# Last stage of an adaLN block on one core: weights stationary and 512 tokens moving in six of seven block products

## Chip, cores and metric

The kernel runs on one core of a Trainium2 chip. The metric is device time in microseconds (us) of one execution; before the change it is 539.46 us, the median of three runs (539.36 to 539.9).

## What is computed

One transformer block on 2048 tokens of width 512, in float32, with a modulation vector from `silu(c) @ w_mod`:

```python
h = _layernorm(x) * (1 + ca) + sa
x = x + ga * _A_ref(h, wqkv, wo)              # linear attention, 32 heads
h = _layernorm(x) * (1 + cb) + sb
x = x + gb * (((h @ w_gate) * (h @ w_up)) @ w_down)   # F = 1376
```

## The kernel before

The work is written out by hand, engine by engine; no scheduler reorders it. Tokens come in four chunks of 512, each as four tiles of 128 tokens by 512 columns (`xts[chunk][j]`). Every matrix operand is split into a high and a low half of type float32r (`split`, L195), and a product of two matrices is three matmuls: high·high, high·low, low·high.

The feed-forward part runs in blocks of 128 hidden features (`block`, L1176). Chunks 2 and 3 have their down projection last, after all blocks, in `Down.run` (L1515), which is the last stage. It multiplies the hidden features of chunks 2 and 3 (`a11`, `a12` of chunk 2, `a21`, `a22` of chunk 3; left and right are even and odd feature tiles) by `w_down` (`b11`, `b12`, `b21`, `b22`) by Winograd's form of Strassen's scheme: seven products of blocks instead of eight. Left sums are `s1` to `s4`, right sums `t1` to `t4`. Each product has 5 pairs of feature tiles, three of them a sixth pair of 96 features (`odd`). In the order in which they run, they are called P1 to P7 here:

| product | left, right | pairs |
|---|---|---|
| P1 | a11, b11 | 5 |
| P2 | a12, b21 | 6 |
| P3 | s2, t2 | 5 |
| P4 | s1, t1 | 5 |
| P5 | s3, t3 | 6 |
| P6 | s4, b22 | 6 |
| P7 | a22, t4 | 6 |

Before, the tokens are stationary: for each of the four token tiles of a product, 128 tokens by 128 features sit in the array and the weights' 256 output columns move. P1, P3, P5 and P7 use two PSUM banks (`C`), two token tiles to a bank, with three 256-wide matmuls per pair and tile (`mm`, L1448). P2, P4 and P6 use four banks (`A`) and put high and low weights side by side into one 512-wide matmul, beside one 256-wide one (`mm_wide`, L1458). After each product VectorE adds the PSUM banks to x in SBUF (`add`, L1521); what Winograd's scheme shares between outputs comes out of PSUM by keeping sums in the banks. P7 runs tile by tile in the order j = 0, 2, 1, 3; tiles 0 and 1 share one bank, 2 and 3 the other.

Around the products, `h_split` (L1419) and `h_next` (L1425) make left halves: ScalarE copies a high half (`kh`), VectorE subtracts it for the low half (`kl`); in `h_next` VectorE also forms the s2 or s4 sum just ahead (L1417). Right halves were made in earlier blocks, parked in DRAM, and come back in `w_fetch` (L1395). SP issues every DMA of the kernel in order, and each DMA uses one of eight semaphores in turn, so that at most eight are in flight. Each engine works its queue in order.

`stow` (L996) and the lifts earlier in the kernel already use the way of turning that matters here: VectorE's transpose turns 32x32 blocks, and DMAs through DRAM put blocks in place.

Of the kernel before, what the change touches and what calls it, by code (L numbers as in the profile page):

```python
# [24 lines left out]
def tile_adaln_block(  # L25
# [27 lines left out]
    xv = x[0].rearrange("(c p j) d -> c j p d", p=P, j=NJ)  # L53
    ov = out[0].rearrange("(c p j) d -> c j p d", p=P, j=NJ)
# [56 lines left out]
    def load(src, tag):  # L111
        raw = B(tag, (P, *src.shape[1:]))[:src.shape[0]]
        nc.sync.dma_start(raw, src)
        return raw

    def load_x(ch):
        return [load(xv[ch, j], "x") for j in range(NJ)]
# [823 lines left out]
    def evac(ch, dn, js=range(NJ), last=False, cols=((0, D),)):  # L941
        for j in js:
            xt = xts[ch][j]
            for a, b in cols:
                nc.vector.tensor_tensor(xt[:, a:b], dn[j][:, a:b], xt[:, a:b], op=ALU.add)  # L945
                if last:
                    nc.sync.dma_start(ov[ch, j, :, a:b], xt[:, a:b])
# [214 lines left out]
    def copy(out, x):  # L1162
        nc.scalar.activation(out, x, AF.Copy)  # L1163
# [126 lines left out]
    banks, others = [], []  # L1290
# [18 lines left out]
    def ffn():  # L1309

        m = 0
        for g, (cs, fs) in enumerate(groups):
# [19 lines left out]
        wide_down = Down((2, 3), m, draws.pop(m))  # L1332
        wide_down.planned()
# [14 lines left out]
    class Down:  # L1348

        def __init__(self, cs, m, odd):  # L1350
            self.cs, self.m, self.odd = cs, m, odd
# [4 lines left out]
            self.raw, self.t = {}, {}  # L1356

# [100 lines left out]
        def mm_wide(self, bs, j, pairs, start):  # L1458

            a, b = j * P, (j + 1) * P  # L1460
            for (h, l), w in pairs:
                k = h.shape[0]
                nc.tensor.matmul(bs[j], h[:, a:b], w[:k].rearrange("p t c -> p (t c)"), start=start, stop=False, skip_group_check=True)  # L1463
                nc.tensor.matmul(bs[j][:, :HALF], l[:, a:b], w[:k, 0], start=False, stop=False, skip_group_check=True)
                start = False

        def product(self, bs, js, left, right, start, odd=None):
            pairs = [(self.parts[i][left, "split"], self.w[right, i]) for i in range(self.NI)]
            if odd:
                pairs.append((self.h[LATE[0]][odd[0]], self.w["odd", odd[1]]))  # L1470
            for j in js:
                if len(bs) == NJ:
                    self.mm_wide(bs, j, pairs, start)
                else:
                    self.mm(bs, j, pairs, start and j % 2 == 0)
# [38 lines left out]

        def run(self):  # L1515

            c0, c1 = self.cs
            x = lambda c, half, j: xts[c][j][:, half * HALF:(half + 1) * HALF]
            A, C = banks, others[:2]

            def add(c, half, bs, js, store=None):  # L1521
                for j in js:
                    parts = [bs[j][:, :HALF], bs[j][:, HALF:]] if bs is A else [self.part(bs, j)]
                    for ps in parts:
                        nc.vector.tensor_tensor(x(c, half, j), x(c, half, j), ps, op=ALU.add)
                    if store:
                        a, b = store
                        nc.sync.dma_start(ov[c, j, :, a:b], xts[c][j][:, a:b])

            lo, hi, js = (0, 1), (2, 3), range(NJ)  # L1530
            pairs = range(self.NI)
            last = self.NI - 1
# [305 lines left out]
```

## Time and profile before

| | |
|---|---|
| median of 3 runs | 539.46 us |
| the profiled execution's own time | 539.58 us |
| its span, first to last instruction | 537.9 us |
| last stage, P1's first matmul to P7's last | 478.86 to 534.61 us |
| mean granted TensorE clock | 1.000 |
| VectorE, ScalarE, GpSimd busy | 76%, 55%, 30% of the span |
| DMA | 109.21 MB, mean 203 GB/s |

PE is TensorE's matmul side, PEld its weight loads, DVE VectorE, ACT ScalarE, POOL GpSimd, SP the engine that issues DMAs. In a timeline a row gives start, length, engine, line, operation and tiles, with "xN" for merged neighbours and in brackets the idle time before it and what ended it. A matmul's own length is modelled and overlaps the next one; pace is read from starts. In the row of a group, the first number behind the bar is its busy time, the second the mean length of one in ns.

### The profile page before, as it was taken

What the parts mean: (1) busy time and instruction counts of PE and PEld (TensorE: products, weight loads), DVE (VectorE), ACT (ScalarE), POOL (GpSimd) and SP (SyncE); (2) the same over time, 40 slices, a digit from 0 to 9 for tenths busy, and PEclk for the clock granted to TensorE, in tenths of its full rate; (3) what the DMA queues carried; (4) which work ended last, traced back from release to release, by engine and by line L of the source; (5) the groups of instructions that cost most, each with busy time, mean ns of one, the idle gap of its engine ahead of it and who ended that gap; (6) DMA issues with size and microseconds to landing.
All of it is one profiled execution on the core that took longest, in us unless ns stands there. A gap on an engine that the chain in (4) does not pass through costs nothing.

```text
span 537.9 us, 8026 instructions
## 1 busy us (share of the span) xinstructions
PE 532.6 (99%) x2549; PEld 444.7 (83%) x2549; DVE 408.1 (76%) x701; ACT 297.7 (55%) x564; POOL 160.0 (30%) x170
## 2 busy tenths in 40 slices
PE   8999999999999999999999999999999999999997
PEld 7888888888888878878888888887888888889997
DVE  7997879999989888779766576996556564669772
ACT  3696877648587765577684545454434334246030
POOL 2001010010021220076696577747532322210000
PEclk9999999999999999999999999999999999999999
DMA  8902427310165165947869596794289998689222
GB/s 283 387 35 92 144 98 216 98 60 2 45 195 194 41 209 147 310 143 228 279 197 319 207 323 224 216 372 120 74 300 334 388 389 315 229 278 392 83 77 81
DMA packets 86396, 109.21 MB, mean 203 GB/s; under 512 B 10897, under 2 KB 41617, under 8 KB 86353
## 3 DMA queue, kind: packets, MB, share of 16 engines
q1 hardware_dynamic: 86352, 108.70, 60.3%
q8 instruction: 20, 0.33, 0.3%
q14 instruction: 24, 0.19, 0.1%
HBM read 65.93 MB, written 42.73 MB: 202 GB/s over the span
## 4 chain that ended last, share of the span: by engine, by line
PE 99%; DVE 0%; issue 0%
PE bank L1158 27%; PE acc L875 8%; PE acc L1158 7%; PE acc L1455 6%; PE bank L209 4%; PE bank L211 4%; PE bank L210 4%; PE bank L1463 3%; PE acc L416 3%; PE acc L418 3%; PE acc L417 3%; PE acc L1242 3%; PE acc L1241 3%; PE acc L1243 3%; PE bank L958 2%; PE bank L960 2%
## 5 line engine op out<-in xcount | busy, mean ns | idle before, releaser
L1158 PE MATMUL bank<-h,w 128*128 128x512 f32 (+1 forms) x630 | 145.4, 389 | 0.0
L1158 PEld LDWEIGHTS bank<-h,w 128*128 128x128 f32 (+1 forms) x630 | 117.0, 186 | 26.1 <-DVE u L1220 0.2
L1163 ACT ACTIVATE bank<-bank 128x512 f32<-128x512 f32 (+1 forms) x30 | 17.5, 583 | 74.0 <-PE bank L1158 73.8
L197 DVE TENSOR_TENSOR kl<-u,kh 128x512 fp32r<-128x512 f32 (+1 forms) x38 | 26.3, 736 | 23.9 <-ACT kh L196 21.9
L265 POOL TENSOR_TENSOR rstd<-ve,half 128x2 f32<-128x2 f32 (+3 forms) x13 | 11.8, 911 | 107.8 <-DVE ve L264 44.5
L209 PE MATMUL bank<-w,h 128*128 128x512 f32 x104 | 40.8, 392 | 0.0
L211 PE MATMUL bank<-w,h 128*128 128x512 f32 x104 | 40.6, 391 | 0.0
L210 PE MATMUL bank<-w,h 128*128 128x512 f32 x104 | 40.5, 390 | 0.0
L1158 PE MATMUL acc<-h,w 128*128 128x512 f32 x168 | 38.7, 389 | 0.0
L197 POOL TENSOR_TENSOR w<-raw,w 128x512 fp32r<-128x512 f32 (+1 forms) x15 | 22.2, 1483 | 53.4 <-ACT w L196 47.8
L875 PE MATMUL acc<-w,xh 128*128 128x512 f32 x120 | 37.1, 390 | 0.0
L1158 PEld LDWEIGHTS acc<-h,w 128*128 128x128 f32 x168 | 31.5, 188 | 6.5
L945 DVE TENSOR_TENSOR x<-acc,x 128x512 f32<-128x512 f32 x40 | 26.5, 686 | 12.8 <-PE acc L1243 11.1
L1120 POOL TENSOR_TENSOR w<-raw,w 128x256 fp32r<-128x256 f32 (+3 forms) x22 | 23.9, 1084 | 37.4 <-ACT w L1113 33.2
L1455 PE MATMUL acc<-w,kh 128*128 128x256 f32 (+1 forms) x176 | 31.8, 283 | 0.0
L1120 POOL TENSOR_TENSOR w<-t,w 128x512 fp32r<-128x512 f32 (+1 forms) x22 | 30.2, 1372 | 0.0
L1455 PEld LDWEIGHTS acc<-w,kh 128*128 128x128 f32 (+1 forms) x176 | 27.5, 192 | 0.2
L875 PEld LDWEIGHTS acc<-w,xh 128*128 128x128 f32 x120 | 22.4, 188 | 4.6
L416 PE MATMUL acc<-kh,xh 128*128 128x512 f32 x64 | 25.2, 394 | 0.0
L418 PE MATMUL acc<-kl,xh 128*128 128x512 f32 x64 | 25.0, 391 | 0.0
L417 PE MATMUL acc<-kh,xl 128*128 128x512 f32 x64 | 25.0, 390 | 0.0
L1241 PE MATMUL acc<-w,kh 128*128 128x512 f32 x64 | 24.9, 389 | 0.0
(258 smaller groups left out, 1325.5 us busy)
## 6 DMA issues: line engine op xcount, KB each, us to landing
right<-w SPq DMA_DIRECT2D x56, 256.0 KB, 3.6
w<-right SPq DMA_DIRECT2D x56, 256.0 KB, 5.1
raw<-in_w_mod_dram SPq DMA_DIRECT2D x24, 256.0 KB, 3.9
raw<-in_B_w_down_dram SPq DMA_DIRECT2D x20, 256.0 KB, 4.2
down_t<-w SPq DMA_DIRECT2D x20, 256.0 KB, 5.1
w<-down_t SPq DMA_DIRECT2D x20, 256.0 KB, 5.4
x<-in_A_x_dram SPq DMA_DIRECT2D x16, 256.0 KB, 5.6
down_b<-w SPq DMA_DIRECT2D x15, 256.0 KB, 5.1
```

The lines of the kernel that those rows point to most:

```text
L197: (low or nc.vector).tensor_tensor(l, src, f32(h), op=ALU.subtract)
L209: nc.tensor.matmul(ps, ah, bh, start=i == 0, stop=False)
L210: nc.tensor.matmul(ps, ah, bl, start=False, stop=False)
L211: nc.tensor.matmul(ps, al, bh, start=False, stop=i == n - 1)
L416: nc.tensor.matmul(tacc[k], xh[:, a:b], kh, start=first, stop=False)
L417: nc.tensor.matmul(tacc[k], xl[:, a:b], kh, start=False, stop=False)
L418: nc.tensor.matmul(tacc[k], xh[:, a:b], kl, start=False, stop=last)
L875: nc.tensor.matmul(yps[i], x, y, start=False, stop=k == KD - 1 and x is al, skip_group_check=True)
L1120: sub = lambda out, x, y: (on or nc.gpsimd).tensor_tensor(out, x, f32(y), op=ALU.subtract)
L1158: mm = lambda x, y, **kw: nc.tensor.matmul(ps, x[:, k], y, skip_group_check=True, **kw)
L1241: nc.tensor.matmul(ps, hh[:, a:b], dh[:n, c:d], start=i == 0, stop=False)
L1455: nc.tensor.matmul(ps, x[:, a:b], y, start=start, stop=False, skip_group_check=True)
```

## The change

P1 to P6 are turned round: the weights are stationary, 128 output columns by 128 features, and all 512 tokens of the chunk move. The 256 columns of an output block are two sets, the even and the odd columns (`m` = 0 and 1; the stationary operand takes every second column of the weight tile). A product is then, for each set, three 512-wide matmuls per pair, into one bank: `sets[0]` are the four `acc` banks, `sets[1]` the four `bank` banks, and a, b, c, d name four banks of each. All eight banks are in use.

Winograd's sums stay in PSUM or go to SBUF instead of being added to x one by one: after P1 ScalarE copies bank a to bank b, and P2 adds onto a (output block c11), P3 onto b (u2). After P3 b is copied to c, and a and b to SBUF; P4 goes into d, copied to SBUF (p5); P5 adds onto c, copied to SBUF (u3) and added to p5; P6 adds onto d, which is added to u2.

Results now have columns on partitions. `flip` turns each with four VectorE transposes of 128x256 (32x32 blocks, writing every second element), and `move` stores or loads a 128x512 tile with four DMAs of 64 KB, in runs of 64 floats. So that x has the same form, chunks 2 and 3 keep their tokens in another order (the view `tokens`), x is stored to DRAM (`x_store`, eight DMAs in earlier blocks) and reloaded in blocks (`x_blocks`, 24 DMAs); `finish` adds and stores an output block. Block u3 is stored to DRAM and reloaded as rows (c21), since P7 stays as it was and adds to x by token tiles. `mm_wide` is gone.

```diff
-    xv = x[0].rearrange("(c p j) d -> c j p d", p=P, j=NJ)
-    ov = out[0].rearrange("(c p j) d -> c j p d", p=P, j=NJ)
+    def tokens(of):
+        strided, whole = (of[0].rearrange(v, p=P, j=NJ) for v in ("(c p j) d -> c j p d", "(c j p) d -> c j p d"))
+        return lambda ch, j: (strided if ch < 2 else whole)[ch, j]
...
+        def turned(self, bank, left, right, fresh, odd=None):
+
+            for m in range(2):
+                ps, start = sets[m][bank], fresh
+                for (h, l), w in self.pairs(left, right, odd):
+                    k = h.shape[0]
+                    of = w[:k].rearrange("p t (r m) -> p t m r", m=2)[:, :, m]
+                    for x, y in ((0, h), (0, l), (1, h)):
+                        nc.tensor.matmul(ps, of[:, x], y, start=start, stop=False, skip_group_check=True)
+                        start = False
+            self.drop(left, right)
...
+            for n, c in enumerate(self.cs):
+                for j in range(NJ):
+                    put(2 * n + j // 2 - 3, "p2", lambda c=c, j=j: self.x_store(c, j))
...
+        def blocks_of(self, rows, half, u):
+
+            cols = rows[u * HALF:(u + 1) * HALF, half * HALF:(half + 1) * HALF]
+            return cols.rearrange("(b i) (q f) -> q i b f", i=BL, q=NQ)
+
+        def move(self, t, of, out):
+            for q in range(NQ):
+                sb = t[q * BL:(q + 1) * BL].rearrange("i (b f) -> i b f", f=2 * BL)
+                nc.sync.dma_start(*((of[q], sb) if out else (sb, of[q])))
...
+        def flip(self, ys):
+
+            out = []
+            for u in range(2):
+                t = B("t")
+                for m in range(2):
+                    nc.vector.transpose(t.rearrange("p (b e m) -> p b e m", m=2, e=BL)[..., m],
+                                        ys[m][:, u * HALF:(u + 1) * HALF].rearrange("p (b i) -> p b i", i=BL))
+                out.append(t)
+            return out
+
+        def finish(self, ts, c, half):
+            rows = out[0][c * CH:(c + 1) * CH]
+            for u, (t, xb) in enumerate(zip(ts, self.xb.pop((c, half)))):
+                nc.vector.tensor_tensor(t, t, xb, op=ALU.add)
+                self.move(t, self.blocks_of(rows, half, u), True)
...
-            self.product(C, js, "a11", "b11", True)
-            self.drop("a11", "b11")
+            self.turned(a, "a11", "b11", True)
             self.h_next("s2", 0, 1)
-            add(c0, 0, C, js)
+            for m in both:
+                copy(sets[m][b], sets[m][a])
             self.w_fetch("t1")
-            self.product(A, js, "a12", "b21", True, (0, 0))
-            self.drop("a12", "b21")
+            self.turned(a, "a12", "b21", False, (0, 0))
             self.h_next("s2", 2, 3, 4)
-            add(c0, 0, A, js)
             self.w_fetch("t3")
-            self.product(C, js, "s2", "t2", False)
-            self.drop("s2", "t2")
+            self.turned(b, "s2", "t2", False)
             self.h_split("s1", *pairs)
-            add(c0, 1, C, js)
+            c11 = to_sbuf(a)
+            for m in both:
+                copy(sets[m][c], sets[m][b])
+            u2 = to_sbuf(b)
             self.w_fetch("b22")
-            self.product(A, js, "s1", "t1", True)
-            self.drop("s1", "t1")
+            self.turned(d, "s1", "t1", True)
+            self.x_blocks(c0, 0)
             self.h_split("s3", *pairs)
             self.h_next("s4", 0)
-            add(c1, 1, A, js)
+            p5 = to_sbuf(d)
             self.w_fetch("t4")
-            self.product(C, js, "s3", "t3", False, (1, 1))
-            self.drop("s3", "t3")
+            self.turned(c, "s3", "t3", False, (1, 1))
+            self.x_blocks(c1, 1)
+            self.x_blocks(c0, 1)
             self.h_next("s4", 1, 2, 3, 4)
-            add(c1, 1, C, js, (HALF, D))
-            self.product(A, js, "s4", "b22", False, (0, 1))
-            self.drop("s4", "b22")
             self.h_split("a22", *pairs)
-            add(c0, 1, A, js, (0, D))
+            c11 = self.flip(c11)
+            u3 = self.flip(to_sbuf(c))
+            c21 = tc.dram_tile([CH, D], F32, name="c21")
+            for u, t in enumerate(u3):
+                self.move(t, self.blocks_of(c21, 0, u), True)
+            p5 = self.flip(onto(c, p5))
+            self.finish(c11, c0, 0)
+            u3 = [load(c21.rearrange("(j p) d -> j p d", p=P)[j][:, :HALF], "u") for j in js]
+            self.turned(d, "s4", "b22", False, (0, 1))
+            self.finish(p5, c1, 1)
+            u2 = self.flip(onto(d, u2))
+            x = lambda j: xts[c1][j][:, :HALF]
+            for j in js:
+                nc.vector.tensor_tensor(x(j), x(j), u3[j], op=ALU.add)
+            self.finish(u2, c0, 1)
...
             before = []
             for j in (0, 2, 1, 3):
-                self.product(C, (j,), "a22", "t4", False, (1, "turn"))
-                add(c1, 0, C, before, (0, HALF))
+                self.product(C, (j,), "a22", "t4", (1, "turn"))
+                add(*before)
                 before = (j,)
-            add(c1, 0, C, before, (0, HALF))
+            add(*before)
```

Three places show what moved. The first is ScalarE's queue around the end of P1, before the change: two high halves of a12, then the five of s2 (`kh<-u`, L1431).

```order
L196 ACTIVATE kh_5306<-u_5050 128x512
L196 ACTIVATE kh_5310<-u_5222 128x512
L1431 ACTIVATE kh_5385<-u_4325 128x512
L1431 ACTIVATE kh_5390<-u_4585 128x512
L1431 ACTIVATE kh_5457<-u_4771 128x512
```

After the change the same place has the two bank copies (acc and bank, L1166 of the new kernel) behind the first two halves of s2.

```order
L199 ACTIVATE kh_5316<-u_5060 128x512
L199 ACTIVATE kh_5320<-u_5232 128x512
L1436 ACTIVATE kh_5365<-u_4335 128x512
L1436 ACTIVATE kh_5370<-u_4595 128x512
L1166 ACTIVATE acc_4542<-acc_4541 128x512
L1166 ACTIVATE bank_2874<-bank_2873 128x512
L1436 ACTIVATE kh_5423<-u_4781 128x512
```

The copy of `acc_4541`, the bank of P1 and P2, comes third behind work on s2. In the same way six copies (`u<-acc`, `u<-bank`, `acc<-acc`, `bank<-bank`, `u<-acc`, `u<-bank`) now stand between the high halves of s1 and those of s3.

The second place is the end of VectorE's queue. Before, it held the adds of P6 (banks) and then those of P7, in the order 0, 2, 1, 3.

```order
L1525 TENSOR_TENSOR x_152<-x_152,bank_2875 128x256 x2
L1525 TENSOR_TENSOR x_154<-x_154,bank_2876 128x256 x2
L1525 TENSOR_TENSOR x_156<-x_156,acc_4531 128x256
L1525 TENSOR_TENSOR x_160<-x_160,acc_4532 128x256
L1525 TENSOR_TENSOR x_158<-x_158,acc_4531 128x256
L1525 TENSOR_TENSOR x_162<-x_162,acc_4532 128x256
```

Now the last twelve rows are two turns of u2 (L1557), the adds of the reloaded u3 (L1630), the adds of u2's output block (L1565), and P7's adds.

```order
L1557 STREAM_TRANSPOSE t_5794<-u_5503 128x256
L1557 STREAM_TRANSPOSE t_5794<-u_5504 128x256
L1630 TENSOR_TENSOR x_156<-x_156,u_5735 128x256
L1630 TENSOR_TENSOR x_158<-x_158,u_5737 128x256
L1630 TENSOR_TENSOR x_160<-x_160,u_5739 128x256
L1630 TENSOR_TENSOR x_162<-x_162,u_5741 128x256
L1565 TENSOR_TENSOR t_5791<-t_5791,x_5643 128x512
L1565 TENSOR_TENSOR t_5794<-t_5794,x_5648 128x512
L1635 TENSOR_TENSOR x_156<-x_156,acc_4541 128x256
L1635 TENSOR_TENSOR x_160<-x_160,acc_4542 128x256
L1635 TENSOR_TENSOR x_158<-x_158,acc_4541 128x256
L1635 TENSOR_TENSOR x_162<-x_162,acc_4542 128x256
```

P7's first add, of `acc_4541`, has moved behind six adds, four of which read tiles that come from DRAM. TensorE's first matmul of tile 1 writes the same bank and waits for that add, as it did before.

The third place is the end of SP's queue. Before, twelve stores of x rows closed it, the last eight being these.

```order
L1528 DMA out_dram<-x_148 128x512
L1528 DMA out_dram<-x_150 128x512
L1528 DMA out_dram<-x_152 128x512
L1528 DMA out_dram<-x_154 128x512
L1528 DMA out_dram<-x_156 128x256
L1528 DMA out_dram<-x_160 128x256
L1528 DMA out_dram<-x_158 128x256
L1528 DMA out_dram<-x_162 128x256
```

Now, behind the last loads of x blocks, stand these twelve rows ("x4" is four DMAs), and after them the four stores of P7 as before.

```order
L1542 DMA c_5708<-t_5702 32x8x64 x4
L1542 DMA c_5708<-t_5705 32x8x64 x4
L1542 DMA out_dram<-t_5692 32x8x64 x4
L1542 DMA out_dram<-t_5695 32x8x64 x4
L116 DMA u_5735<-c_5708 128x256
L116 DMA u_5737<-c_5708 128x256
L116 DMA u_5739<-c_5708 128x256
L116 DMA u_5741<-c_5708 128x256
L1542 DMA out_dram<-t_5719 32x8x64 x4
L1542 DMA out_dram<-t_5722 32x8x64 x4
L1542 DMA out_dram<-t_5791 32x8x64 x4
L1542 DMA out_dram<-t_5794 32x8x64 x4
```

The reload of u3 (`u<-c`) stands behind sixteen small stores, and sixteen more stand between it and P7's stores.

More of the change, by code (lines that the diff above doesn't have):

```diff
@@ L116, in load_x @@
     def load_x(ch):
-        return [load(xv[ch, j], "x") for j in range(NJ)]
+        return [load(xv(ch, j), "x") for j in range(NJ)]
     def load_mod(v):
@@ L1309, in ffn @@
     def ffn():
+        wide_down = Down((2, 3), sum(cs != (2, 3) for cs, f in steps))
         m = 0
+        wide_down.planned()
         for g, (cs, fs) in enumerate(groups):
@@ L1356, in __init__ @@
             self.raw, self.t = {}, {}
+            self.x_rows, self.xb = {}, {}
         def w_split(self, key, src, low=None):
@@ L1456, in mm, with pairs @@
                     start = False
[L1458 to L1467, printed above, removed]
+        def pairs(self, left, right, odd):
             pairs = [(self.parts[i][left, "split"], self.w[right, i]) for i in range(self.NI)]
@@ L1470, in product @@
                 pairs.append((self.h[LATE[0]][odd[0]], self.w["odd", odd[1]]))
+            return pairs
+        def product(self, bs, js, left, right, odd):
             for j in js:
[L1472 to L1475, printed above, removed]
+                self.mm(bs, j, self.pairs(left, right, odd), j % 2 == 0)
+        def turned(self, bank, left, right, fresh, odd=None):
[8 more added lines that the diff above has]
+            self.drop(left, right)
         def drop(self, left, right):
@@ L1513, in planned, with x_store @@
                     put(b, "p4", lambda i=i: self.w_park(i, "t2", "t3", "t4"), lambda: self.w_fetch("b21"))
+        def x_store(self, c, j):
+            half = c != self.cs[0]
+            if c not in self.x_rows:
+                self.x_rows[c] = tc.dram_tile([CH, D], F32, name=f"x_rows_{c}")
+            rows = self.x_rows[c].rearrange("(j p) d -> j p d", p=P)
+            a = HALF if half else 0
+            nc.sync.dma_start(rows[j][:, a:], xts[c][j][:, a:])
+        def blocks_of(self, rows, half, u):
+            cols = rows[u * HALF:(u + 1) * HALF, half * HALF:(half + 1) * HALF]
+            return cols.rearrange("(b i) (q f) -> q i b f", i=BL, q=NQ)
@@ new lines, in move, with x_blocks @@
+        def move(self, t, of, out):
+            for q in range(NQ):
+                sb = t[q * BL:(q + 1) * BL].rearrange("i (b f) -> i b f", f=2 * BL)
+                nc.sync.dma_start(*((of[q], sb) if out else (sb, of[q])))
+        def x_blocks(self, c, half):
+            self.xb[c, half] = []
+            for u in range(2):
+                t = B("x")
+                self.move(t, self.blocks_of(self.x_rows[c], half, u), False)
+                self.xb[c, half].append(t)
+        def flip(self, ys):
+            out = []
+            for u in range(2):
+                t = B("t")
[4 more added lines that the diff above has]
+            return out
@@ L1530, in run, with to_sbuf, onto @@
-            lo, hi, js = (0, 1), (2, 3), range(NJ)
-            pairs = range(self.NI)
-            last = self.NI - 1
+            C, js, pairs, both = others[:2], range(NJ), range(self.NI), range(2)
+            a, b, c, d = range(4)
+            sets.extend((others, banks))
+            last = self.NI - 1
+            def to_sbuf(bank):
+                ys = [B("u") for _ in both]
+                for m in both:
+                    copy(ys[m], sets[m][bank])
+                return ys
+            def onto(bank, ys):
+                for m in both:
+                    nc.vector.tensor_tensor(ys[m], sets[m][bank], ys[m], op=ALU.add)
+                return ys
```

28 lines of the change are left out of this document (12 added, 16 removed).

## The prediction

> **What bounds the kernel now.** I read the busy times first, then the chain that ended last, then the last stage product by product.
>
> ```profile
> span 537.9 us, 8026 instructions
> PE 532.6 (99%) x2549; PEld 444.7 (83%) x2549; DVE 408.1 (76%) x701; ACT 297.7 (55%) x564; POOL 160.0 (30%) x170
> PE 99%; DVE 0%; issue 0%
> ...
> core 0: us, PE busy (x) PEld busy (x) DVE busy (x) ACT busy (x) POOL busy (x), PEclk, DMA share, GB/s
> 478.86:486.05 7.19, 7.19 (x61) 7.19 (x60) 6.89 (x12) 1.74 (x3) 0.00 (x0) 1.00 0.96 322
> 486.05:494.48 8.43, 8.43 (x51) 7.37 (x50) 8.18 (x18) 5.09 (x11) 0.00 (x0) 1.00 1.05 391
> 494.48:501.66 7.18, 7.18 (x63) 7.18 (x61) 4.55 (x10) 2.16 (x5) 0.00 (x0) 1.00 0.70 254
> 501.66:508.73 7.07, 7.07 (x42) 6.13 (x41) 6.68 (x13) 1.22 (x2) 0.00 (x0) 1.00 0.17 65
> 508.73:517.37 8.64, 8.64 (x75) 8.64 (x74) 6.95 (x15) 4.51 (x8) 0.00 (x0) 1.00 0.10 32
> 517.37:525.87 8.50, 8.50 (x51) 7.44 (x50) 6.11 (x13) 0.00 (x0) 0.00 (x0) 1.00 0.29 104
> 525.87:534.61 8.74, 8.70 (x73) 8.50 (x71) 2.11 (x6) 0.00 (x0) 0.00 (x0) 1.00 0.28 97
> ```
>
> The busy line alone doesn't prove that TensorE is the bound; the chain does, with 99% of the span on it. The windows cut the last stage at its seven products, P1 to P7: TensorE is busy in all 55.75 us of them, at full clock. So here a shorter stream of matmuls is worth its full length, and each new wait of TensorE costs its full length too. I count in us from the stage's start, 478.86; P7 ends at 55.75.
>
> **The matmuls themselves.** Starts of neighbouring rows give the pace.
>
> ```profile
> 475.69 3.34 PE L1158 MATMUL bank<-h,w 128*128 128x512 f32 x14
> 478.86 0.40 PE L1455 MATMUL acc<-w,kh 128*128 128x256 f32 x2
> ...
> 479.21 0.40 PE L1455 MATMUL acc<-w,kh 128*128 128x256 f32 x2
> ```
>
> Fourteen 512-wide matmuls from 475.69 to 478.86: 0.227 us each. Three 256-wide ones from 478.86 to 479.21 (0.36 with the next): 0.120 each. P1 to P6 took 47.01 us (525.87 − 478.86). They become 33 pairs × 6 = 198 matmuls of 512: 198 × 0.227 = 44.9. **Gain 2.1 us**; P7 keeps its 72 narrow matmuls (8.7). The new stationary operand takes every second column. No row shows such a weight load. Bounds: free, as it loads beside the matmul before it (the windows have PEld busy 7.19 of 7.19 at a pace of 0.120, so 0.227 leaves nearly twice the room); or the room is overrun and the pace goes to 0.235–0.24, +1.6 to +2.6 us. I take free, since a load would have to be nearly twice as long to show.
>
> **First new wait, before P2.** P2 now accumulates in the bank that P1 left, and ScalarE must copy that bank first. The copy stands behind two high halves of s2.
>
> ```profile
> 484.94 1.24 ACT L1431 ACTIVATE kh<-u 128x512 fp32r<-128x512 f32 x2 [5.09 <-DVE u L1417]
> L1163 ACT ACTIVATE acc<-acc 128x512 f32<-128x512 f32 x8 | 4.7, 582 | 23.8 <-PE acc L1158 23.8
> ```
>
> These two wait for VectorE's s2 sums; nothing ahead of those sums changes, so they again end at 6.08 + 1.24 = 7.3. The copy (0.58) ends at 7.9. P1 ends at 30 × 0.227 = 6.8. **TensorE waits 1.1 us**; everything in P2 to P7 is queued behind it. Bounds: 0.6 (only the copy, were nothing ahead of it) to 1.3 (0.2 of hand-over, as in the 0.23 that VectorE waits for ScalarE in a row below). The second half's copy has until 12, so it is free.
>
> With that, P2 runs 7.9–16.1, P3 to 22.9, P4 to 29.7, P5 to 37.9, P6 to 46.1, and P7's tiles j = 0, 2, 1, 3 take 18 × 0.120 = 2.16 each: j = 1 would start at 50.4.
>
> **Second new wait, inside P7.** Tile 1 shares a bank with tile 0, so it waits until VectorE has added tile 0. That add now stands at the end of a long VectorE queue. Rows for its pieces:
>
> ```profile
> 491.33 2.71 ACT L196 ACTIVATE kh<-s 128x512 fp32r<-128x512 f32 x5
> 481.15 3.10 DVE L197 TENSOR_TENSOR kl<-u,kh 128x512 fp32r<-128x512 f32 x5
> 485.68 0.69 DVE L1433 TENSOR_TENSOR kl<-u,kh 128x512 fp32r<-128x512 f32 x1 [0.23 <-ACT kh L1431]
> 487.49 1.41 DVE L1525 TENSOR_TENSOR x<-x,acc 128x256 f32<-128x256 f32 x4
> 505.54 1.28 DVE L1417 TENSOR_TENSOR u<-u,u 128x512 f32<-128x512 f32 x2
> ...
> 507.59 3.23 DVE L1525 TENSOR_TENSOR x<-x,bank 128x256 f32<-128x256 f32 x8
> ...
> 515.20 0.74 DVE L1525 TENSOR_TENSOR x<-x,acc 128x256 f32<-128x256 f32 x2
> L759 DVE STREAM_TRANSPOSE f<-u 128x512 f32<-128x512 f32 x14 | 9.7, 701 | 0.0
> 173.65 3.80 SPq L334 DMA_DIRECT2D u<-moved  x8
> u<-moved SPq DMA_DIRECT2D x56, 64.0 KB, 2.0
> stowed<-n SPq DMA_DIRECT2D x32, 64.0 KB, 1.8
> out_dram<-x SPq DMA_DIRECT2D x8, 128.0 KB, 1.9
> ```
>
> In a row of equals VectorE takes 0.60 us for 512 columns (3.10 for five) and 0.33 for 256 (1.41 for four); ScalarE 0.54.
>
> - *ScalarE.* The high halves of s3 now stand behind two bank copies and two copies to SBUF that need P3's end (22.9, +0.2): the second bank copy ends at 23.7, the SBUF copies at 24.7, the first high half at 25.3. Before, s3 was ready long ahead.
> - *VectorE from 25.3.* Five lows of s3 to 28.3. The s4 work took 505.54 to 515.20 with 3.2 of adds in it, so 6.4; it gets 0.4 more because two SBUF copies of P4 stand in ScalarE's queue: 35.1. Five lows of a22: 38.2. Then the new work. A turn of 256 columns shows nowhere: from 0.33, as an add of that size, to 0.70, as the whole 512-column turn (701 ns). I take 0.34, because a turn of 512 takes what an add of 512 takes (701 and 0.69). Eight turns: 40.9, the first reloadable tile ready at 40.4. Two sums onto P5's bank 42.1; four turns 43.5; four adds 45.9, the first done at 44.2. Two sums onto P6's bank, the second not before P6's end: 46.9; four turns: 48.3. The next adds need the u3 tiles back from DRAM.
> - *SP.* One 64 KB DMA is issued every 0.48 us (8 in 3.80) and lands after 1.8 to 2.0. Runs of 64 are 256 bytes; no row shows that size. Bounds: at the rate of the second window (391 GB/s) 64 KB take 0.17 us; at a quarter of it 0.67, which is longer than the issue and adds 0.2 for each of 36 DMAs, 7 us. I take the issue as the limit, as for the stowed and moved DMAs of the same 64 KB. From 40.4: eight c21 stores to 44.3, eight stores of c11 to 48.1, then four reloads, the last issued at 49.6 and landed (2.0) at 51.6.
> - *VectorE again.* The fourth x add ends at 52.0, two adds of u2 at 53.2, tile 0's add at 53.6. TensorE has waited since 50.4: **3.2 us**. Tiles 1 and 3 then run to 57.9; tile 2's add is long done.
>
> **The end.** Before, the last add ended at 535.03 and its store was issued at once.
>
> ```profile
> 534.61 0.42 DVE L1525 TENSOR_TENSOR x<-x,acc 128x256 f32<-128x256 f32 x1 [1.73 <-PE acc L1455]
> 532.90 2.49 SPq L1528 DMA_DIRECT2D out_dram<-x  x2
> ```
>
> That row ends at 535.39; less the 0.33 of one issue the last store began at 535.06, or 56.2. Now the last add ends at 58.4, but SP is still issuing: after the reloads (50.0) eight stores of p5 to 53.9, eight of u2 to 57.8, then four stores of P7, the last at 59.2. So SP adds **0.8**. The landing (1.9) is as before.
>
> What lies beside other work is costed at nothing. TensorE's waits of the whole execution fill one row:
>
> ```profile
> PE acc L146 <- DVE w L141: 2.0, 1, 2.0
> ```
>
> So the weight loads behind which the eight x_rows stores are put, four to ten blocks ahead of the stage, come early enough today; were that cover gone, each store would cost its 0.48 of SP. The 24 loads of x blocks take 11.5 us of SP, from about 14 to 28, when the DMA share is 0.70 and then 0.17; t4, queued between them, is due only at 46. ScalarE's twelve copies (7 us) fit in its idle half, apart from the two places named.
>
> **Sum:** −2.1 + 1.1 + 3.2 + 0.8 = +3.0 us against the profiled execution's own 539.58 (span 537.9 and 1.7 around it; the median of the runs, 539.46, is 0.02% below): **542.6**.
>
> **One more danger: the clock.**
>
> ```profile
> 2.01 8.11 PE L146 MATMUL acc<-w 128*128 128x512 f32 x24 [2.01 <-DVE w L141]
> ```
>
> After the idle start, 24 matmuls took 8.11 us where 0.227 each would be 5.4: half as long again. If a wait of 3.2 us brought that back, the 4.3 us of tiles 1 and 3 would take 6.4: +2.1, 544.7. The windows of the stage all show 1.00, and no row before has an idle stretch of TensorE like this one. The Trainium skill ("TensorE: Matmul & The Clock Gate", Part 1) says that an idle window of about 3.4 us puts the array back to half clock. By that rule a wait of 3.2 us just escapes and the sum stays 542.6; a wait some tenths longer would give the 544.7. No run here shows it yet.
>
> **The rivals.**
> - *The added work stays off TensorE's path* (faster). It decides at two points: the bank copy done by 6.8, tile 0's add by 50.4. Then the gain of 2.1 remains: 537.5. For it: VectorE and ScalarE have idle time in every window. Against it: the order of their queues, 1.1 late at the first point by rows that don't change. Chance 0.06.
> - *The reload is early.* If u3 is back by 48.3 (fewer stores ahead of it in effect), tile 0's add is done at 48.3 + 4 × 0.33 + 1.3 + 0.4 = 51.3; the wait is 0.9, and with SP out of the way: −2.1 + 1.1 + 0.9 = −0.1, 539.5. Against it: 16 issues at 0.48 stand between first turn and reload. Chance 0.10.
> - *Forecast*, 541.3 to 544.0 with small errors in every term: 0.58.
> - *Turns cost a full 0.70.* Twelve before the first add of c11: 12 × 0.36 = 4.3 later for reload and all behind it: 546.9. Chance 0.10.
> - *Strided weights or 256-byte runs are slow.* Weights: +2.6, partly under the second wait, about 544.5; runs: up to 549.6. Chance 0.11.
> - *The clock drops*, 544.7: 0.05.
> - That the stage does not change as told is excluded by the order of instructions.
>
> **How the numbers follow.** The range reaches from 540.3 (most of the early-reload case left out) to 546.4 (full-price turns and slow runs left out): about 0.2 outside. About 0.2% (1.1 us) is what a measurement of this kernel can tell from no change. Faster by more: the first rival, 0.06. Within: early reload and the forecast's low edge, 0.11. Slower by more: 0.83.
>
> **What would show it.** 512-wide matmuls of P1–P6 at 0.227 with no gap inside a product: the gain; a gap of about 1.1 us before P2, ended by ScalarE's bank copy; a gap of about 3 us before P7's third tile, ended by VectorE; SP issuing without pause from c21 to the end. Wrong would be: no gap in P7 (the queue model fails), a pace over 0.23 (weights), turns near 0.7, or a wait in P3 to P6 that I have not seen.

## The result and the profile after

The changed kernel takes **546.31 us** (median of 4 runs, 545.35 to 546.88) against 539.68 before (4 runs of the same comparison): 1.012 times as long, 95% interval 1.0103 to 1.0138. The forecast, 542.6, had the sign and the places of the two waits; the loss is 6.6 us instead of 3.1. The profiled execution took 546.24.

First the page: the spans, the busy line, and the chain that ended last.

```profile
span 544.5 us, 7854 instructions
PE 534.6 (98%) x2419; PEld 441.4 (81%) x2419; DVE 407.0 (75%) x695; ACT 303.4 (56%) x576; POOL 158.9 (29%) x170
PE 93%; DVE 3%; SPq 1%; DMA 1%; issue 1%; ACT 0%; DVEq 0%; ACTq 0%
```

TensorE's share of the chain went from 99% to 93%; VectorE, SP's queue and a DMA have taken the rest. TensorE's busy time even rose, though it has 130 matmuls fewer. Now the windows of the last stage, product by product; P7 is cut at 535.5 (columns as in the windows of before).

```profile
478.77:486.67 7.90, 7.17 (x32) 5.60 (x30) 7.62 (x13) 2.41 (x5) 0.00 (x0) 1.00 1.00 339
486.67:495.17 8.50, 8.50 (x36) 7.13 (x37) 6.90 (x12) 5.32 (x10) 0.00 (x0) 1.00 1.05 394
495.17:502.17 7.00, 7.00 (x31) 5.80 (x30) 0.00 (x0) 1.18 (x2) 0.00 (x0) 1.00 0.85 198
502.17:509.17 7.00, 7.00 (x31) 5.79 (x30) 4.58 (x8) 5.11 (x10) 0.00 (x0) 1.00 0.75 219
509.17:517.59 8.42, 8.42 (x38) 6.98 (x36) 7.93 (x14) 6.16 (x12) 0.00 (x0) 1.00 0.28 63
517.59:526.00 8.41, 8.41 (x38) 6.98 (x37) 8.01 (x19) 0.60 (x1) 0.00 (x0) 1.00 0.41 87
526.00:535.50 9.50, 5.51 (x42) 5.31 (x41) 5.59 (x13) 0.00 (x0) 0.00 (x0) 0.86 0.62 146
535.50:541.00 5.50, 5.50 (x32) 5.50 (x32) 0.42 (x1) 0.00 (x0) 0.00 (x0) 0.62 0.66 166
```

The stage begins at 478.77 (478.86 before), so nothing was lost ahead of it. P3 and P4 have 30 matmuls each in 7.00 us: **0.233 us** apiece, not 0.227. And in the last two rows the granted clock is 0.86 and 0.62. TensorE's two gaps, from its timeline:

```profile
485.54 0.40 PE L1481 MATMUL bank<-kh,w 128*128 128x512 f32 x1
486.67 0.51 PE L1481 MATMUL acc<-kh,w 128*128 128x512 f32 x1 [0.73 <-ACT acc L1166]
...
530.19 0.28 PE L1460 MATMUL acc<-w,kl 96*128 96x256 f32 x1
534.46 0.79 PE L1460 MATMUL acc<-w,kh 128*128 128x256 f32 x2 [3.99 <-DVE x L1635]
```

Both stand where they were forecast, with the releasers that were forecast: ScalarE's bank copy before P2, VectorE's add of tile 0 before tile 1. By pace, P1 is over at 478.77 + 30 × 0.2333 = 485.77 and tile 2 at 530.19 + 0.12 = 530.31, so the waits are 0.9 and 4.1 (the brackets, 0.73 and 3.99, count from the modelled ends). Behind the second, windows cut where the clock steps:

```profile
529.40:532.80 3.40, 1.07 (x9) 0.86 (x8) 1.63 (x5) 0.00 (x0) 0.00 (x0) 1.00 0.79 211
532.80:536.20 3.40, 1.74 (x8) 1.74 (x9) 1.94 (x5) 0.00 (x0) 0.00 (x0) 0.50 0.61 130
536.20:539.60 3.40, 3.40 (x18) 3.40 (x18) 0.42 (x1) 0.00 (x0) 0.00 (x0) 0.50 0.61 132
539.60:542.00 2.40, 1.68 (x14) 1.48 (x13) 0.42 (x1) 0.00 (x0) 0.00 (x0) 0.99 0.45 150
```

The clock falls to half at 532.8, 2.5 us after TensorE ran out of work, and stays there for 6.8 us. In the third row TensorE works through, at half clock; the fourth is back at full clock. From tile 1's first matmul to the end of tile 3's last, which starts at 541.00, it is 541.12 − 534.46 = 6.7 us instead of 36 × 0.120 = 4.3 (P7 has six pairs, so 18 matmuls a tile; four products have a sixth pair, as the table of products shows, not three).

The terms of the sum, in us:

| term | forecast | measured |
|---|---|---|
| P1 to P6, without the wait: 47.01 before | −2.1 | 46.33: −0.7 |
| wait before P2 | +1.1 | +0.9 |
| wait before P7's tile 1 | +3.2 | +4.1 |
| half clock in tiles 1 and 3, to the start of the last add (541.32) | 0 (a rival at +2.1) | +2.4 |
| from there to the start of the last store (541.77): 0.45 before, 0.45 now | +0.8 | 0.0 |
| sum (of the unrounded terms) | +3.0 | +6.8 |

The spans differ by 6.6: the stage began 0.09 earlier, and the end behind the last store is 0.1 shorter.

### The profile page after: what moved, and what is told of

Read it like the earlier page. It is cut to its first block, busy times and chain, and to the rows that moved or that the text cites. A ratio compares the mean times of both kernels' runs of the same rounds, so it can differ in the third digit from the quotient of the medians.

```text
span 544.5 us, 7854 instructions
## 1 busy us (share of the span) xinstructions
PE 534.6 (98%) x2419; PEld 441.4 (81%) x2419; DVE 407.0 (75%) x695; ACT 303.4 (56%) x576; POOL 158.9 (29%) x170
## 4 chain that ended last, share of the span: by engine, by line
PE 93%; DVE 3%; SPq 1%; DMA 1%; issue 1%; ACT 0%; DVEq 0%; ACTq 0%
PE bank L1161 26%; PE acc L878 8%; PE acc L1161 7%; PE bank L212 4%; PE bank L214 4%; PE bank L213 4%; PE acc L419 3%; PE acc L421 3%; PE acc L420 3%; PE acc L1246 3%; PE acc L1244 3%; PE acc L1245 3%; PE acc L1481 2%; PE bank L963 2%; PE bank L961 2%; PE bank L962 2%
## 5 line engine op out<-in xcount | busy, mean ns | idle before, releaser
L1166 ACT ACTIVATE bank<-bank 128x512 f32<-128x512 f32 (+1 forms) x32 | 18.6, 582 | 76.9 <-PE bank L1161 73.8
L214 PE MATMUL bank<-w,h 128*128 128x512 f32 x104 | 40.7, 391 | 0.0
L1166 ACT ACTIVATE u<-bank 128x512 f32<-128x512 f32 (+1 forms) x36 | 21.3, 593 | 6.9 <-PE bank L1481 3.4
L1246 PE MATMUL acc<-w,kl 128*128 128x512 f32 x64 | 24.9, 389 | 0.0
```

Source lines behind the costliest of these rows:

```text
L214: nc.tensor.matmul(ps, al, bh, start=False, stop=i == n - 1)
L1246: nc.tensor.matmul(ps, hl[:, a:b], dh[:n, c:d], start=False, stop=i == len(hs) - 1)
```

## The experiments

Theory: the changed kernel loses by three separate things, a slower pace of the turned matmuls, VectorE's and SP's queues in P7, and the half clock that the resulting wait brings. The rivals to each are in the expectations. Where a time is given "from the stage's start", that run's own first matmul of P1 is zero, since it lies between 478.4 and 480.2 from run to run.

### The wait filled with work: 17 matmuls, and 4

```diff
             for j in (0, 2, 1, 3):
+                if j == 1:
+                    for _ in range(17):
+                        nc.tensor.matmul(sets[1][a], self.w["t4", 0][:, 0, :P], self.parts[0]["a22", "split"][0],
+                                         start=True, stop=True, skip_group_check=True)
                 self.product(C, (j,), "a22", "t4", (1, "turn"))
```

> Seventeen 512-wide matmuls into a free PSUM bank are put ahead of P7's third tile, where TensorE waits 4.0 us in the changed kernel; their result is read by nobody. Theory A (the long wait lets the clock fall): tiles 1 and 3 then take 36 x 0.120 = 4.3 us instead of 6.8 and the granted clock stays 1.00. The wait for VectorE's add still ends near 534.4. The last add comes 2.5 earlier, but SP, which starts P7's stores at 538.56 and issues one every 0.5, issues the last at 540.05 instead of 541.77: total 1.7 less, 544.6. Theory B (the slow tiles come of the stores that run beside them): tiles 1 and 3 still take 6.8, total unchanged at 546.3.

Measured: 545.11 us (543.95 to 545.38). TensorE's and SP's timeline rows, and the window of tiles 1 and 3:

```profile
530.96 4.04 PE L1642 MATMUL bank<-kh,w 128*128 128x512 f32 x17
535.27 0.51 PE L1460 MATMUL acc<-w,kh 128*128 128x256 f32 x2 [0.27 <-DVE x L1635]
...
539.22 1.89 SPq L1636 DMA_DIRECT2D out_dram<-x  x4
...
535.90:539.80 3.90, 3.90 (x33) 3.74 (x32) 0.42 (x1) 0.00 (x0) 0.00 (x0) 1.00 0.60 126
```

The wait ends as late as before (535.27, with a stage start 0.63 later), but the clock stays at 1.00 and the two tiles take 4.4 us. The transfers beside them are the same, so theory B falls: it is the idle stretch. The end came only 1.7 us earlier from the stage's start, as expected (the medians differ by 1.2): SP's four stores of P7 now follow one another without a pause, so SP holds the end.

> As the run with seventeen, but four matmuls (0.9 us), so that TensorE stands idle for 3.2 us instead of 4.1 before P7's third tile. If the clock falls only after an idle stretch of 3.4 us or more: no fall, tiles 1 and 3 in 4.3, total 544.6. If an idle stretch of 3 us is enough: tiles 1 and 3 in about 6.8, total 546.3. If the slow tiles have another cause: 6.8 as well, and seventeen matmuls do not help either.

Measured: 545.43 us (545.06 to 547.75). The row of tile 1's first matmul, and the windows, cut where the clock steps:

```profile
534.42 0.80 PE L1460 MATMUL acc<-w,kh 128*128 128x256 f32 x2 [3.37 <-DVE x L1635]
...
530.70:534.10 3.40, 0.35 (x2) 0.00 (x0) 2.68 (x7) 0.00 (x0) 0.00 (x0) 1.00 0.78 173
534.10:537.50 3.40, 3.08 (x14) 3.08 (x15) 0.59 (x2) 0.00 (x0) 0.00 (x0) 0.50 0.62 131
537.50:540.40 2.90, 2.83 (x24) 2.63 (x22) 0.45 (x2) 0.00 (x0) 0.00 (x0) 1.00 0.72 201
```

TensorE idled for 3.4 us by its row and the clock fell, but for one stretch of 3.4 us instead of two. Neither number of the expectation came out: tiles 1 and 3 took 5.8 us. The rows together fit a rule in steps of 3.4 us. The clock fell after a stretch with TensorE busy for 1.07 us (changed kernel) and 0.35 us (here) of 3.40; a stretch at half clock that was busy for 1.74 was followed by another, one busy for 3.08 was not. That the stretches lie on a grid of their own, not counted from the end of the work, is seen from the falls: 2.5 us after the work's end in one run, 3.2 in the other. The clock records of the traces bear the grid out: the clock rose at 7.14 us and fell at 532.80 in the changed kernel, and at 5.01 and 534.08 here, which is 154 and 155 times 3.413. The Trainium skill ("TensorE: Matmul & The Clock Gate", Part 1) describes free-running windows of about 3.4 us; these rows agree with that. It asks for an idle window; here a window with 31% of work in it was enough.

How many stretches a wait costs therefore depends on where it lies on the grid, and not on its length alone. The mean granted clock of the four runs of the changed kernel is 0.994, 0.997, 0.994 and 0.993, the 0.997 in the fastest (545.35); with four matmuls it is 0.997 three times and 0.993 in the slowest (547.75). One stretch at half clock takes 3.4 × 0.5 / 544 = 0.003 off that mean. Only one run of each has a trace, so where the stretches lay in the others isn't known.

### Neighbouring columns as the stationary operand

```diff
-                    of = w[:k].rearrange("p t (r m) -> p t m r", m=2)[:, :, m]
+                    of = w[:k].rearrange("p t (m r) -> p t m r", m=2)[:, :, m]
```

> The stationary operand takes columns 0 to 127 and 128 to 255 instead of the even and the odd ones, one after the other in SBUF; the output columns come out in another order than the reference's. Theory A (the stride of two costs 0.007 us per matmul): pace 0.227 in P1 to P6 instead of 0.234, the six products 1.3 us shorter; the end hardly moves (0 to 0.3 less, 546.0 to 546.3), since the wait in P7 is set by VectorE and SP, grows by 1.0 and keeps the clock low. Theory B (it is the moving operand, or the change of weights for every matmul): pace stays 0.234.

Measured (one run): 546.56 us. The first matmuls of P4 and of P5:

```profile
502.21 0.39 PE L1481 MATMUL acc<-kh,w 128*128 128x512 f32 x1
...
509.01 0.39 PE L1481 MATMUL acc<-kh,w 128*128 128x512 f32 x1
```

Thirty matmuls in 6.80 us, 0.2267 instead of 0.2333. Theory A holds: the stride of two costs 0.0066 us per matmul, 198 × 0.0066 = 1.3 us. The rows of the weight loads show where it lies, in the changed kernel first, then here:

```profile
L1481 PEld LDWEIGHTS bank<-kh,w 128*128 128x128 f32 x60 | 11.6, 193 | 2.4
L1481 PEld LDWEIGHTS bank<-kh,w 128*128 128x128 f32 x60 | 11.3, 188 | 2.4
```

A load of every second column takes 193 ns, one of neighbouring columns 188: by these rows most of the 6.6 ns is in the load, and a longer load shows in the pace although the load engine is idle for about 40 ns of every matmul in both runs. The end didn't come earlier: TensorE arrives earlier at the same wait, which grows to 4.8, and the clock falls for two stretches again.

### A bank for each of P7's tiles

```diff
-            return bs[j // 2][:, j % 2 * HALF:(j % 2 + 1) * HALF]
+            return bs[j][:, :HALF]
...
-            C, js, pairs, both = others[:2], range(NJ), range(self.NI), range(2)
+            C, js, pairs, both = others[:2] + banks[:2], range(NJ), range(self.NI), range(2)
...
-                self.mm(bs, j, self.pairs(left, right, odd), j % 2 == 0)
+                self.mm(bs, j, self.pairs(left, right, odd), True)
```

> Each of P7's four token tiles gets a PSUM bank of its own, so tile 1 needn't wait for VectorE's add of tile 0. The queue theory: TensorE has no wait in P7, P7 takes 72 x 0.120 = 8.6 and ends near 534.7, clock 1.00; VectorE adds tile 0 at 534.4 as before and tile 3 by 535.6; then SP alone sets the end, with its last store issued at 540.05 instead of 541.77: 544.6. Rival (SP isn't a bound, only the wait is): the last store is issued at 536, total 540.6.

Measured: 544.87 us (544.71 to 545.53). VectorE's last add and SP's last stores:

```profile
535.49 0.42 DVE L1635 TENSOR_TENSOR x<-x,bank 128x256 f32<-128x256 f32 x1
...
538.73 1.88 SPq L1636 DMA_DIRECT2D out_dram<-x  x4
```

TensorE ends P7 at 534.4 and VectorE adds the last tile by 535.9; still the last store starts only at 540.2, because SP is working off its queue. So taking TensorE's wait of 4 us and the half clock away (6.5 us of TensorE's time) brings 1.4: the wait hid a second bound of nearly the same length. The rival, SP not being a bound, falls.

### The first bank copy ahead of s2

```diff
+            copy(sets[0][b], sets[0][a])
             self.h_next("s2", 0, 1)
-            for m in both:
-                copy(sets[m][b], sets[m][a])
+            copy(sets[1][b], sets[1][a])
```

> ScalarE's copy of P1's first bank goes ahead of the two high halves of s2, the copy of the second stays behind them. P1's first bank is complete half-way through P1, so the queue theory has P2 start without a wait: the 0.9 us at that place goes. ScalarE's later copies wait for P3's end, so the whole chain from the s3 halves to the add of tile 0 comes 0.9 earlier with it, and so does the end: 545.4. The wait in P7 stays at about 4.1 and the clock still falls there. Rival: VectorE's queue, not TensorE, sets that chain; then P7's wait grows by 0.9 and the total stays at 546.3.

Measured: 545.21 us (544.5 to 546.15). ScalarE's first copy, the first turns on VectorE, SP's stores of c11, and the one wait of TensorE that is left in the stage:

```profile
482.67 0.58 ACT L1166 ACTIVATE acc<-acc 128x512 f32<-128x512 f32 x1 [2.72 <-PE acc L1481]
...
516.54 2.73 DVE L1557 STREAM_TRANSPOSE t<-u 128x256 f32<-128x256 f32 x8
...
522.60 5.36 SPq L1542 DMA_DIRECT2D out_dram<-t  x8
...
PE acc L1460 <- DVE x L1635: 4.7, 1, 4.7
```

The copy is done at 483.25, 2.7 us before P2 begins (485.97), and the wait before P2 is gone. The turns begin 1.1 us earlier from the stage's start (37.6 instead of 38.6), so VectorE's chain does hang on TensorE there, as the theory said. But tile 0's add came only 0.3 earlier: the rest went in SP's stores of c11 (5.36 instead of 5.01) and in later landings of the reload. So the wait before P2 goes, as the theory said, but the wait in P7 grows from 4.0 to 4.7, nearly as the rival said. The median is 1.1 lower, and this profiled execution (546.15, the slowest of the four) shows hardly any of it. Whether the end gains isn't settled: the four runs (544.5 to 546.15) overlap those of the changed kernel (545.35 to 546.88), and three of them have a mean clock of 0.997, against one of the changed kernel's four, so part of the 1.1 can be the clock's.

### Block c11 early

```diff
             self.x_blocks(c0, 0)
+            self.finish(self.flip(c11), c0, 0)
             self.h_split("s3", *pairs)
...
-            c11 = self.flip(c11)
...
-            self.finish(c11, c0, 0)
```

> The turns and the x adds of output block c11, with its eight stores, go ahead of the high halves of s3 in the program, into the 10.8 us in which VectorE is idle before them. The queue theory: VectorE turns u3 right when ScalarE has copied it, SP stores c21 near 519.2 and issues the reloads near 523.1 instead of 528.6, VectorE's add of tile 0 ends near 531.1 instead of 534.4; TensorE waits 0.8 instead of 4.0 before tile 1 and the clock stays at 1.00; P7 ends near 535.6, SP's last store is issued near 536.3: total 5.5 less, 540.8. Rival (VectorE's adds of u2 and the landing of the reload are the bound, not SP's stores of c11): tile 0's add comes 1 us earlier at most, total 543 to 545.

Measured: 541.37 us (9 runs, 540.66 to 542.28), 1.0027 times before, 1.0017 to 1.0037. TensorE's waits in the stage, and SP's end:

```profile
PE acc L1481 <- ACT acc L1166: 0.7, 1, 0.7
PE acc L1460 <- DVE x L1634: 0.6, 1, 0.6
...
523.16 2.06 SPq L116 DMA_DIRECT2D u<-c  x4
...
534.87 1.87 SPq L1635 DMA_DIRECT2D out_dram<-x  x4
```

One block moved into VectorE's idle time returns 4.9 of the 6.6 us. The reloads are issued from 523.16 instead of 528.58, the wait before tile 1 falls from 4.0 to 0.6, and the clock stays at 1.00. Its rival falls. The edit moves VectorE's turns of c11 as well as SP's stores, but SP begins the stores of c21 only 0.5 earlier from the stage's start (40.2 instead of 40.7) and the reloads 5.6 earlier (44.2 instead of 49.8): nearly all of it is SP's stores of c11, which stood ahead of the reload.

### The three edits together

Own banks, early copy and early c11, as in the three diffs above.

> Three edits at once: the first bank copy early, block c11 early, a bank for each of P7's tiles. If TensorE's two waits and the clock are all that the turned form lost besides its stride, TensorE runs without a wait: 198 x 0.2335 + 72 x 0.120 = 54.9 instead of before's 55.75, SP has issued u2's stores by then, and the total is 0.8 below before's 539.7: 538.9 (539.6 if an instruction load again holds SP's stores up by 1.2). Rival: SP's 36 small DMAs are a bound of their own: 540.5 to 541.

Measured: 540.04 us (10 runs, 539.42 to 541.49), 1.0003 times before, 0.9994 to 1.0013. SP's last stores:

```profile
534.56 1.88 SPq L1635 DMA_DIRECT2D out_dram<-x  x4
```

TensorE runs the stage without a wait, in 54.9 us from first to last matmul as worked out, and still the kernel is only level with before, not 0.8 ahead of it. The last store starts 55.8 us from the stage's start, 0.4 earlier than before's 56.2, since SP issues up to the end: the rival is right that SP is a bound of its own, though not on its price (540.5 to 541). The median lies 0.6 above the 539.4 that this gives; this execution's stage began at 480.2, 1.4 later than before's. Of that, 0.9 is there after 23 us of the kernel and the rest by 173 us, far ahead of the edits; 0.4 comes from TensorE's first 24 matmuls, which take 8.49 us instead of 8.11, as the clock rises at 7.96 instead of 7.09. Where the other 1.0 comes from is open.

### Columns reordered when the weights are split

```diff
             w = B("w", (P, 2, HALF), F32R)[:n]
-            nc.scalar.activation(w[:, 0], src, AF.Copy)
-            (low or nc.vector).tensor_tensor(w[:, 1], src, f32(w[:, 0]), op=ALU.subtract)
+            h, l = w[:, 0], w[:, 1]
+            if key[0] != "t4" and key[1] != "turn":
+                src = src.rearrange("p (r m) -> p m r", m=2)
+                h, l = (x.rearrange("p (m r) -> p m r", m=2) for x in (h, l))
+            nc.scalar.activation(h, src, AF.Copy)
+            (low or nc.vector).tensor_tensor(l, src, f32(h), op=ALU.subtract)
             self.w[key] = w
...
-                    of = w[:k].rearrange("p t (r m) -> p t m r", m=2)[:, :, m]
+                    of = w[:k].rearrange("p t (m r) -> p t m r", m=2)[:, :, m]
```

> The run before, and the weights' high and low halves are written with their even columns first, so that the stationary operand is 128 neighbouring columns (reads of every second element on ScalarE and GpSimd in the earlier blocks instead). Pace 0.227 instead of 0.2335: 1.3 us less, 537.6; 0.9 of it is lost again if SP's stores then end last: 538.5. Rival: the strided reads slow ScalarE's or GpSimd's splits enough to hold TensorE up in the blocks ahead of the stage: the stage starts later, 539 or more.

Measured: 538.88 us (10 runs, 538.42 to 539.83), 0.9982 times before, 0.9973 to 0.9992. The three edits of the run before are in it as well. The last add and SP's last stores:

```profile
533.16 0.42 DVE L1638 TENSOR_TENSOR x<-x,bank 128x256 f32<-128x256 f32 x1 [1.74 <-PE bank L1464]
...
532.94 1.89 SPq L1639 DMA_DIRECT2D out_dram<-x  x4
```

The matmuls' pace is 0.227, and TensorE's part of the stage 53.6. A split on ScalarE takes 430 ns with the strided read, 416 in the changed kernel, and GpSimd's 754 instead of 751; TensorE has no new wait in the whole kernel, so the rival falls. The last add is done at 533.58, the last store starts at 534.42: SP's end costs 0.8.

### ScalarE issues u2's stores

```diff
-                nc.sync.dma_start(*((of[q], sb) if out else (sb, of[q])))
+                (nc.scalar if out == "act" else nc.sync).dma_start(*((of[q], sb) if out else (sb, of[q])))
...
-            self.finish(u2, c0, 1)
+            self.finish(u2, c0, 1, "act")
```

(`finish` hands the word on to `move`.)

> The run with reordered weights, and ScalarE, idle by then, issues the eight stores of u2 in place of SP. In the run before, the last add of P7 ended at 533.58 and SP, issuing without a pause, began the last store at 534.42. If SP's queue sets the end there, the last store now begins right after the last add: 0.8 less, 538.1. Rival: two engines that issue DMAs slow each other, or the transfers themselves are the bound: 538.9 as before or more.

Measured: **538.16 us** (6 runs, 537.71 to 538.73), 0.9968 times before, 0.9956 to 0.998: faster than both kernels, and than before by 0.3%. The chain of the page, and the end of SP, ScalarE and VectorE:

```profile
PE 99%; DVE 0%; issue 0%
...
529.72 4.50 SPq L1639 DMA_DIRECT2D out_dram<-x  x4
...
528.79 4.14 ACTq L1546 DMA_DIRECT2D out_dram<-t  x8
...
533.44 0.42 DVE L1638 TENSOR_TENSOR x<-x,bank 128x256 f32<-128x256 f32 x1 [1.74 <-PE bank L1464]
```

SP's four stores of P7 spread over 4.5 us, each at once when its tile is added; the last starts at 533.89, behind the add that ends at 533.86. The chain is TensorE's again, at 99%. From the stage's start the last store begins at 54.3, 1.9 earlier than before: the whole gain of 2.1 that the first term of the forecast had, less 0.2.

## Why the prediction was wrong

The sign, the places of both waits and their releasers came out; the size did not. Against the forecast the pace took 1.4 us more, the second wait 0.9 and the clock 2.4; the first wait gave 0.2 back and the end 0.8. The 546.31 still lies inside the range of 540.3 to 546.4, and that is luck: strided weights (about 544.5) and the clock (544.7) were priced as rivals one at a time, and both came.

**"198 × 0.227 = 44.9. Gain 2.1": mis-sized.** The step that failed is "I take free, since a load would have to be nearly twice as long to show". The weight loads' busy share says nothing of the kind: in P4 they are busy for 5.79 of 7.00 us, and the pace is still 0.2333. The run with neighbouring columns has 0.2267 with nothing else changed, and a load that is only 5 ns longer by its row already shows. The upper price offered (0.235 and more) was nearly right, and a pace over 0.23 was among the signs of being wrong; the term is −0.7.

**The first new wait: right.** 0.9 instead of 1.1, ended by the copy, removed by moving the copy.

**The second new wait: right in place and cause, 0.9 too short.** VectorE's add of tile 0 ended at 55.6 from the stage's start, not 53.6, and TensorE came to the wait at 51.5, 1.1 later than taken, by the slower pace. VectorE's rows of the turns and of the last reloaded tile, SP's rows, and one row of SP from the chain of waits:

```profile
517.40 2.72 DVE L1557 STREAM_TRANSPOSE t<-u 128x256 f32<-128x256 f32 x8
532.45 0.42 DVE L1630 TENSOR_TENSOR x<-x,u 128x256 f32<-128x256 f32 x1 [0.22 <-DMA u<-c]
...
519.50 3.87 SPq L1542 DMA_DIRECT2D c<-t  x8
523.47 5.01 SPq L1542 DMA_DIRECT2D out_dram<-t  x8
528.58 1.83 SPq L116 DMA_DIRECT2D u<-c  x4
...
526.96 1.52 SPq L1542
```

The 2.0 are 0.4 (the turns begin at 38.6, not 38.2), 1.2 in SP's queue and 0.4 in the landing of the last reload (issued at 530.03, here at 532.4). The turns' price was right, 0.34 for each of eight, and so was SP's 0.48 per issue: eight take 3.87. The next eight take 5.01, and 1.1 of the difference is one issue of 1.52 us, named nowhere in the forecast; see the last section.

**"A wait of 3.2 just escapes": wrong, and the largest miss.** The clock was given 0.05 and cost 2.4. Two things failed. By the prediction's own words the edge was some tenths away, less than the error of a sum of so many queue terms, so the chance was far too small; and the length was taken as what decides. The runs show stretches of 3.4 us on a grid of their own: in the traced executions a wait of 3.4 us (four matmuls) cost one stretch at half clock (tiles 1 and 3 in 5.8 instead of 4.3), one of 4.0 cost two (6.7). The clock fell 2.5 us into the wait of the changed kernel, so at that place a wait of 3.2 would not have escaped either. Seventeen matmuls into the gap removed it.

**The end, "SP adds 0.8": hidden, not wrong.** With tiles 1 and 3 slow, SP has caught up by the time the last add is done. As soon as the clock stays up (seventeen matmuls) or TensorE doesn't wait (own banks), SP sets the end: 0.4 and 4.3 us between last add and last store.

**Costed at nothing, rightly:** the x_rows stores (stage start 478.77 against 478.86; in the nine experiments it lies between 0.4 earlier and 1.4 later), the x loads, ScalarE's other copies (no wait in P3 to P6), and the runs of 256 bytes: stores of such runs land after 1.8 us (median), as the 64 KB stores of before, so the rival that they are slow falls. The loads of x blocks land after 2.8, beside other traffic, and TensorE has no wait from them.

The added work could have stayed off TensorE's path (a rival at 0.06): the last run does it by order, banks, the layout of the weights and a second issuing engine, with no less work.

## What to carry to other kernels

- When a change makes TensorE wait, ask for the clock as well as the length: in the traced executions a wait of 3.4 us cost 1.4 more and one of 4.0 cost 2.4 more, and where the wait lies on the grid can change that from run to run. Filling the gap with unused matmuls shows which part is clock.
- A wait removed on one engine is worth only the distance to the next bound: here TensorE's 6.5 us returned 1.4 until SP's queue was shortened too. Put late results into the idle time of the engine that makes them, and order a queue by who waits for it, the reload ahead of stores that nobody waits for.
- A strided operand can be paid where it is read 198 times on the bound engine, or where it is written once on an idle one.

## What was not expected of the hardware

**Loads of instructions and stalls of SP's DMAs come together.** The DMA queues between 526.8 and 528.4 in the changed kernel:

```profile
q1 hardware_dynamic: 547, 0.13, 39.5%
q8 instruction: 1, 0.02, 4.6%
...
out_dram<-t SPq DMA_DIRECT2D x2, 64.0 KB, 2.9
```

In these 1.6 us one packet of 0.02 MB of instructions is moved beside 547 packets of data; the stores begun just before land after 2.9 us (the last number) instead of 1.8, and the issue at 526.96 takes 1.52 instead of 0.46. All nine experiments have such a long issue (1.4 to 1.9 us) beside such a load between 525 and 528. Where the load falls, the stall falls: with c11 early, the early stores met a load at about 502 in the run with three edits and took 2.86 for four; in the run with reordered weights the load came at 499.5, ahead of them, and eight took 3.85.

```profile
502.02 2.86 SPq L1542 DMA_DIRECT2D out_dram<-t  x4
```

```profile
501.49 3.85 SPq L1546 DMA_DIRECT2D out_dram<-t  x8
```

The kernel before has such a load too, at 525.88: a store of 256 KB that SP issued at 524.80 landed after 4.05 us, where the two ahead of it took 2.4, but SP's next issue, at 526.89, took 0.33, with no other store close behind. That the load is the cause is inferred from this coincidence; no run moved it by itself, and which engine's instructions they are isn't shown.

**The turn.** VectorE's transpose of 128x256 costs 0.34 us, as an add of that size (0.33), also when it writes every second element: 2.72 us for eight.
